# A long-convolution and feed-forward kernel: the last convolution step's loads move to GpSimd's queue and are untied from the weights' loads

## The chip, the cores and the metric

One Trainium2 chip, one core. A kernel's time is the device time of one launch in microseconds; the median of several runs is given. The profile is that of one further execution, with the hardware profiler on.

## The reference

The input `x` has 2048 positions of 576 features. It is normalised over the features, and the normalised rows go two ways; both results are added to `x`.

```python
xn = _layernorm(x, axis=-1)
return x + _A_ref(xn, ...) + _B_ref(xn, B_w1, B_w2)
```

`_A_ref` is a long convolution over the positions. Its kernel `K` (2048 taps for each feature) is a sum over 128 complex exponentials; the convolution is done with transforms of twice the length, and `u * Dskip` is added. `_B_ref` is a feed-forward layer:

```python
h = jnp.einsum("bsd,df->bsf", x, w1)     # 576 -> 4608
h = _silu(h)
out = jnp.einsum("bsf,fd->bsd", h, w2)   # 4608 -> 576
```

## The kernel before

**The main stream** is the feed-forward layer (`ffn`). The positions are 16 tiles of 128 rows, `j` = 0 to 15, in two halves of eight; each half is two blocks of four tiles. The 4608 hidden features are 9 chunks (`NCH`) of four tiles of 128. For each half, chunk and block, `up` (L283 to L301) makes the hidden tiles `gh` and `gl` from `w1`, and `down` (L303 to L325) multiplies them with `w2` into `po` in PSUM (three buffers, pool `ps2`), which VectorE adds to the running result `acc[j]` (L320). Precision is kept by splitting each operand in a high and a low part, so each product is three matmuls, and each weight tile, once loaded, is split by ScalarE (high part) and VectorE (low part).

**Weights.** `load_w1` (L240) loads two hidden tiles of `w1` into `w1r`, of which there is one buffer, with three DMAs (L247 to L249); `split_w1` makes `w1h` (ScalarE, L260) and `w1l` (VectorE, L262). `load_w2` (L265, DMA at L269) loads one tile of `w2` into `w2r`, two buffers; `split_w2` makes `w2h` (L278) and `w2l` (L280). A table in `ffn` says after which step of a block the next chunk's weights are loaded and split. Apart from the first, all these loads are in SyncE's queue. A load whose buffer is still being read waits in the queue, and what stands behind it waits too.

**The side stream** (`side`) is the convolution, cut into steps that `weave` places between the steps of the main stream at given fractions of its length. The convolution's transforms end with `spectral`, which stores 32 slices `yo` of its result to the DRAM tensor `d2` (L705, GpSimd's queue). Every row block of `d2` that is read later has rows of all 32 slices, so the first read waits for the last store.

**The last convolution step** is what the change touches. For each tile `j`, `conv_load` (L757) reads 256 rows of `d2` into a tile `ys` of 128 partitions by 4 by 288 floats, with two DMAs of 64 partitions each (L761); there are 8 buffers of `ys` (`AHEAD + 2`, `AHEAD` being 6). `add_conv` (L764) multiplies `ys` with the small matrix `s4` into two PSUM tiles `py` (L774), and VectorE adds them to the destination (L780). For tiles 0 to 7 the feed-forward result had been put aside in DRAM (`dr0`, L323); `load_r0` (L714, DMA at L716) reads it back, two tiles at a time, into `r0` (the profile's `r`), four buffers; after `add_conv` of an odd tile, `store` writes the pair out with four DMAs in GpSimd's queue (L171). For tiles 8 to 15 `add_conv` adds to `acc[j]` directly, in `down` of the last chunk (L307 to L309).

**Order around the change.** `tail` (L710) lists its steps with their places: the loads for tiles 0 to 7 from 0.895 of the main stream on, each 0.0045 after the one before; the eight `last` steps, each with the load for a later tile, from 0.922 on. Each runs under `behind(pins["load"])`: the scheduler may issue the step's instructions only after the weights' load that was built last (`load_w1` and `load_w2` put their DMA there). Within an engine's queue the schedule is fixed when the kernel is built. Each of SyncE's and GpSimd's kinds of DMA has eight semaphores in turn, so a DMA also waits until the eighth DMA before it in its kind has landed.

Of the kernel before, what the change touches and what calls it, by code (L numbers as in the profile page):

```python
# [17 lines left out]
P = 128  # L18
# [23 lines left out]
def kernel(  # L42
# [21 lines left out]
    nc = tc.nc  # L64
    FT = 4
# [17 lines left out]
    dr0 = dram.tile([8 * P, D], F32, name="dr0")  # L83
# [48 lines left out]
    pins = {}  # L132

    def behind(ins):
        return tc.issue_after(ins) if ins is not None else nullcontext()
# [32 lines left out]
    def store(t, j, engines):  # L168

        for ps, v, eng in quarters(ov, engines):  # L170
            eng.dma_start(v[:, j:j + 2] if len(t.shape) > 2 else v[:, j], t[ps])  # L171
# [61 lines left out]
    def ffn():  # L233
        w2v = w2.rearrange("(t p) d -> p t d", p=P)
# [5 lines left out]
        def load_w1(half, c, t):  # L240

            f = c * FT + t
            first = half == 0 and c == 0
            r1 = (pa if first and t else wp).tile([P, 5, 2 * P], F32, tag="w1r", name="w1r", bufs=1)
            fs = slice(f * P, (f + 2) * P)
            eng = nc.gpsimd if first and t == 0 else nc.sync
            eng.dma_start(r1[:, 0:4, :], w1[0:512, fs].rearrange("(k p) f -> p k f", p=P))  # L247
            eng.dma_start(r1[0:64, 4, :], w1[512:576, fs])
            pins["load"] = eng.dma_start(r1[64:128, 4, :], w1[512:576, fs]).ins  # L249
            R1[half, c, t] = r1  # L250

        def split_w1(half, c, t):
# [12 lines left out]
        def load_w2(half, c, t):  # L265

            first = half == 0 and c == 0
            r2 = (pa if first and t > 1 else wp).tile([P, D], F32, tag="w2r", name="w2r", bufs=2)
            pins["load"] = nc.sync.dma_start(r2, w2v[:, c * FT + t, :]).ins  # L269
            R2[half, c, t] = r2  # L270

        def split_w2(half, c, t):
# [30 lines left out]
        def down(blk, jj):  # L303
            half, c, b = blk
            j = 8 * half + 4 * b + jj
            js = slice(jj * P, (jj + 1) * P)
            if half == 1 and c == NCH - 1:  # L307
                conv_load(j + AHEAD)
                add_conv(j, acc[j])  # L309
            for h in range(2):  # L310
                hs = slice(h * HD, (h + 1) * HD)
                po = ps2.tile([P, 512], F32, tag="ps2", name="po")
                n = 0
                for t in range(FT):
                    for g, w in ((0, 0), (0, 1), (1, 0)):
                        pins["pe"] = nc.tensor.matmul(po[:, :HD], G[blk, t][g][:, js], W2[half, c, t][w][:, hs],  # L316
                                                      start=n == 0, stop=n == 3 * FT - 1).ins
                        n += 1
                with tc.high_priority():
                    nc.vector.tensor_add(acc[j][:, hs], po[:, :HD], acc[j][:, hs])  # L320
            if half == 0 and c == NCH - 1:
                rows = slice(j * P, (j + 1) * P)
                nc.sync.dma_start(dr0[rows, :], acc[j])  # L323
                if j % 2:
                    acc[7 + j], acc[8 + j] = load_x(7 + j, accp, "acc", (nc.sync,))  # L325
# [21 lines left out]
        for t in (0, 2):  # L347
            load_w1(0, 0, t)
        for t in (0, 2):
            split_w1(0, 0, t)  # L350
        for t in range(FT):
            load_w2(0, 0, t)
# [10 lines left out]
        for i, blk in enumerate(blocks):  # L363
            half, c, b = blk
            later = i + 1 < len(blocks)
            new = (half, c + 1) if c + 1 < NCH else (half + 1, 0)
            more = new[0] < 2
            if half == 0 and c == NCH - 1:
                next_xt(b)

            after = {
                (0, "u0"): [(load_w1, 0)],
                (0, "u1"): [(split_w1, 0), (load_w2, 0), (load_w2, 1)],
                (0, "u2"): [(load_w1, 2)],
                (1, "u0"): [(split_w1, 2), (split_w2, 0), (load_w2, 2)],
                (1, "d3"): [(split_w2, 1), (load_w2, 3), (split_w2, 2)],
                (1, "u2"): [(split_w2, 3)],
            }
            for step in ("u0", "d0", "d1", "d2", "d3", "u1", "u2", "u3"):
                k = int(step[1])  # L380
                if step[0] == "d":
                    down(blk, k)
                    yield 3.0
                elif later:
                    up(blocks[i + 1], k)
                    yield 3.0
                for f, t in after.get((b, step), ()) if more else ():
                    f(*new, t)
                if half == 0 and c == NCH - 1:
                    for kt in {"d3": (0, 1), "u1": (2, 3), "u2": (4,)}.get(step, ()):  # L390
                        split_xt(b, kt)
# [318 lines left out]
    def tail():  # L710

        r0s = {}

        def load_r0(j):  # L714
            r0s[j] = yp.tile([P, 2, D], F32, tag="r0", name="r0", bufs=4)
            nc.sync.dma_start(r0s[j], dr0[j * P:(j + 2) * P, :].rearrange("(i p) d -> p i d", p=P))  # L716

        def last(j):
            conv_load(j + AHEAD, 8)
            add_conv(j, r0s[j - j % 2][:, j % 2, :])  # L720
            if j % 2:
                store(r0s[j - 1], j - 1, (nc.gpsimd,))

        steps, at = [], tail_at[0]
        for j in range(8):
            for f in (conv_load, load_r0)[:2 - j % 2]:
                steps.append((at, f, j))
                at += tail_at[1]
        steps += [(tail_at[2] + j * tail_at[3], last, j) for j in range(8)]
        for at, f, j in sorted(steps, key=lambda v: v[0]):  # L730
            yield at
            with behind(pins["load"]):
                f(j)

    yss = {}

# [20 lines left out]
    def conv_load(j, first=0):  # L757
        if first <= j < NJ:
            yss[j] = yp.tile([P, 4, HD], F32, tag="ys", name="ys", bufs=AHEAD + 2)
            for h in range(2):  # L760
                nc.sync.dma_start(yss[j][64 * h:64 * h + 64],  # L761
                                  d2[j * 256:(j + 1) * 256, h * HD:(h + 1) * HD].rearrange("(q r) d -> r q d", q=4))

    def add_conv(j, dst):  # L764

        ys = yss.pop(j)
        py = [pss.tile([P, 512], F32, tag="pss", name="py") for _ in range(2)]
        first = pins["pe"]
        for n in range(8):
            q1, q2, h = n // 4, n // 2 % 2, 1 - n % 2  # L770
            o = 64 * q1 + 32 * q2
            rows = slice(64 * h, 64 * h + 64)
            with tc.high_priority() if n else nullcontext(), behind(first):
                mm = nc.tensor.matmul(py[h][o:o + 32, :HD], s4[rows], ys[rows, 2 * q2 + q1],  # L774
                                      start=True, stop=True, tile_position=(64 * h, o), skip_group_check=True)
            if n == 0:
                first = mm.ins
        for h in range(2):
            hs = slice(h * HD, (h + 1) * HD)
            nc.vector.tensor_add(dst[:, hs], py[h][:, :HD], dst[:, hs])  # L780
# [5 lines left out]
    def side():  # L786
# [40 lines left out]
        with tc.tile_pool(name="kl", bufs=2) as kl:  # L827
            for at in spectral():
                yield marks[1] + (at - 1) * (marks[2] - marks[1])
        yp = ctx.enter_context(tc.tile_pool(name="yp", bufs=3))  # L830
        yield from tail()

    sd = side()
# [87 lines left out]
```

## Time and profile before

| | |
|---|---|
| Median of three runs | 1129.19 us (1126.59 to 1129.72) |
| Profiled execution, its own time | 1131.96 us |
| Span of the profile, first to last instruction | 1130.2 us |
| Instructions | 22881 |
| Granted TensorE clock, mean | 0.996 of full speed |
| TensorE matmul busy | 1106.7 us, 98% |
| VectorE, ScalarE, GpSimd busy | 917.1, 708.7, 78.5 us |
| DMA queue q1 (SyncE), share of the 16 engines | 37.6%, 112.07 MB |
| DMA queue q0 (GpSimd), share | 9.4%, 34.14 MB |
| `ys` loads, `r` loads | 32 of 288 KB, 4 of 576 KB |

The profile names engines PE (TensorE), PEld (its weight loads), DVE (VectorE), ACT (ScalarE), POOL (GpSimd) and SP (SyncE). Register, branch, semaphore and DMA-issuing instructions are not counted as busy. A tile name stands without its buffer number, `out<-in`. All times inside a run are counted from the span's start. "SPq" and "POOLq" are the queues of the two engines that issue DMAs; an issue's time is the time the issuing engine takes over it, not that of the transfer. In the queue views, `q1 hardware_dynamic` is what SyncE issued and `q0 software_dynamic` what GpSimd issued; the columns are packets, MB and the share of 16 engines' time. Releasers are inferred: a wait for several things is put down to the last.

The moved DMAs run from 1028.5 to 1091.9 us of the span, its last tenth.

### The profile page before, as it was taken

To read this page: it belongs to the slowest core of one execution; us is meant where nothing else is said; L and a number is where in the kernel's file an instruction comes from. 1 tells how busy PE (TensorE), PEld (TensorE's weight loads), DVE (VectorE), ACT (ScalarE), POOL (GpSimd) and SP (SyncE) were. 2 spreads that over 40 slices of the span, in tenths; PEclk is the share of its full clock that TensorE was granted. 3 is DMA by queue.
4 is the path that set the end of the run, shared out by engine and by line. 5 is a ranking of instruction groups with operands and counts; after the bars stand their busy time and mean duration, and the time that the engine had idled before them with its cause. 6 is when DMAs were issued, how large, how long until landed. Compare 5 with 4: busy or idle time off the path is not lost.

```text
span 1130.2 us, 22881 instructions
## 1 busy us (share of the span) xinstructions
PE 1106.7 (98%) x9144; PEld 998.7 (88%) x9144; DVE 917.1 (81%) x1545; ACT 708.7 (63%) x1229; POOL 78.5 (7%) x130
## 2 busy tenths in 40 slices
PE   6999899999999999999999999999999999999998
PEld 5988799898888989999889998999999999998776
DVE  6698899999999999999999936887778778774433
ACT  4665356767677676676766727787777787772211
POOL 1110100000000000010000000000000000000110
PEclk9999899999999999999999999999999999999999
DMA  9346531334242625254743345554445455336971
GB/s 272 116 121 173 150 86 57 82 107 106 93 105 70 145 65 116 83 124 153 205 152 88 88 86 170 168 164 130 144 142 168 128 169 149 110 104 168 251 189 56
DMA packets 174971, 148.56 MB, mean 131 GB/s; under 512 B 110944, under 2 KB 141680, under 8 KB 174736
## 3 DMA queue, kind: packets, MB, share of 16 engines
q1 hardware_dynamic: 164768, 112.07, 37.6%
q0 software_dynamic: 9712, 34.14, 9.4%
q8 instruction: 72, 1.18, 0.4%
q10 hardware_dynamic: 384, 0.89, 0.3%
q14 instruction: 35, 0.29, 0.1%
HBM read 102.53 MB, written 44.61 MB: 130 GB/s over the span
## 4 chain that ended last, share of the span: by engine, by line
PE 86%; DVE 5%; DMA 5%; SPq 1%; issue 1%; ACT 0%; POOL 0%; DVEq 0%; POOLq 0%; ACTq 0%
PE po L316 36%; PE ph L291 30%; PE kp L631 3%; PE ph L292 3%; PE ph L293 2%; PE pk L754 2%; PE pu L754 2%; PE pb L754 2%; DMA w1r<-in_B_w_dram 2%; PE z L646 2%; PE pu L153 1%; DMA xj<-in_A_u_dram 1%; PE py L774 1%; PE pu L154 1%; DMA d1k<-stage 1%
## 5 line engine op out<-in xcount | busy, mean ns | idle before, releaser
L316 PE MATMUL po<-w2h,gh 128*128 128x288 f32 x1152 | 338.8, 297 | 6.4 <-DVE acc L320 5.7
L316 PE MATMUL po<-w2h,gl 128*128 128x288 f32 x1152 | 338.5, 297 | 1.0 <-DVE gl L301 1.0
L316 PE MATMUL po<-w2l,gh 128*128 128x288 f32 x1152 | 339.4, 296 | 0.0
L316 PEld LDWEIGHTS po<-w2h,gh 128*128 128x128 f32 x1152 | 216.1, 188 | 16.5 <-DVE acc L320 7.0
L316 PEld LDWEIGHTS po<-w2l,gh 128*128 128x128 f32 x1152 | 216.8, 188 | 4.3
L316 PEld LDWEIGHTS po<-w2h,gl 128*128 128x128 f32 x1152 | 216.5, 189 | 3.5 <-DVE gl L301 1.5
L299 ACT ACTIVATE gf<-ph 128x512 f32<-128x512 f32 (+1 forms) x148 | 86.5, 584 | 140.1 <-PE ph L293 124.7
L320 DVE TENSOR_TENSOR acc<-po,acc 128x288 f32<-128x288 f32 x288 | 126.3, 451 | 47.9 <-PE po L316 46.3
L291 PE MATMUL ph<-xh,w1h 128*128 128x512 f32 (+1 forms) x592 | 163.3, 391 | 0.5 <-ACT xh L123 0.5
L291 PE MATMUL ph<-xl,w1h 128*128 128x512 f32 (+1 forms) x592 | 161.5, 388 | 0.0
L291 PE MATMUL ph<-xh,w1l 128*128 128x512 f32 (+1 forms) x592 | 160.1, 386 | 0.0
L301 DVE TENSOR_TENSOR gl<-gf,gh 128x512 fp32r<-128x512 f32 (+1 forms) x148 | 98.7, 670 | 41.3 <-ACT gh L300 40.6
L291 PEld LDWEIGHTS ph<-xh,w1l 128*128 128x128 f32 x592 | 108.5, 189 | 20.1
L291 PEld LDWEIGHTS ph<-xl,w1h 128*128 128x128 f32 x592 | 108.5, 190 | 19.7
L291 PEld LDWEIGHTS ph<-xh,w1h 128*128 128x128 f32 x592 | 106.0, 191 | 20.0 <-issue 3.3
L300 ACT CAST gh<-gf 128x512 fp32r<-128x512 f32 (+1 forms) x148 | 89.5, 609 | 13.4 <-PE po L316 10.5
L278 ACT CAST w2h<-w2r 128x576 fp32r<-128x576 f32 x72 | 46.9, 672 | 30.6 <-PE po L316 19.5
L588 ACT ACTIVATE c<-th,magic 128x1040 f32<-128x1040 f32 x36 | 42.0, 1166 | 33.7 <-DVE C L611 25.7
L262 DVE TENSOR_TENSOR w1l<-w1r,w1h 128x640 fp32r<-128x640 f32 x72 | 56.9, 819 | 4.4 <-ACT w1h L260 4.3
L280 DVE TENSOR_TENSOR w2l<-w2r,w2h 128x576 fp32r<-128x576 f32 x72 | 53.4, 750 | 7.4 <-ACT w2h L278 7.2
L590 ACT ACTIVATE c<-th 128x1040 f32<-128x1040 f32 x36 | 38.7, 1076 | 32.6 <-DVE th L589 32.6
L292 PE MATMUL ph<-x,w1h 128*128 128x512 f32 (+1 forms) x148 | 57.2, 386 | 0.0
(182 smaller groups left out, 1836.9 us busy)
## 6 DMA issues: line engine op xcount, KB each, us to landing
w2r<-in_B_w_dram SPq DMA_DIRECT2D x72, 288.0 KB, 3.4
w1r<-in_B_w_dram SPq DMA_DIRECT2D x35, 512.0 KB, 3.9
d1u<-u POOLq DMA_DIRECT2D x32, 288.0 KB, 2.5
d1k<-stage SPq DMA_DIRECT2D x18, 512.0 KB, 7.7
ur<-d1u SPq DMA_DIRECT2D x32, 288.0 KB, 3.9
kr<-d1k SPq DMA_DIRECT2D x32, 288.0 KB, 2.8
d<-yo POOLq DMA_DIRECT2D x32, 288.0 KB, 3.9
ys<-d SPq DMA_DIRECT2D x32, 288.0 KB, 10.5
```

The source lines that it names most:

```text
L262: pins["w1l"] = nc.vector.tensor_sub(l1, src, h1).ins
L278: pins["w2h"] = nc.scalar.copy(h2, r2).ins
L280: nc.vector.tensor_sub(l2, r2, h2)
L291: nc.tensor.matmul(ph, w[:, kt, :], v[:, kt, a:e], start=n + kt == 0, stop=False)
L292: nc.tensor.matmul(ph, h1[:, 4, :], x4[:, a:e], start=False, stop=False)
L299: nc.scalar.activation(gf, ph, AF.Silu)
L300: pins["gh"] = nc.scalar.copy(gh, gf).ins
L301: pins["gl"] = nc.vector.tensor_sub(gl, gf, gh).ins
L316: pins["pe"] = nc.tensor.matmul(po[:, :HD], G[blk, t][g][:, js], W2[half, c, t][w][:, hs], start=n == 0, stop=n == 3 * FT - 1).ins
L320: nc.vector.tensor_add(acc[j][:, hs], po[:, :HD], acc[j][:, hs])
L588: nc.scalar.activation(c65, th, AF.Identity, bias=magic)
L754: nc.tensor.matmul(dst, st, mv[:, hs], start=n == 0, stop=n == 3 * len(terms) - 1)
```

## The change

All 32 `ys` loads and the four `r0` loads are issued by GpSimd instead of SyncE. The steps of `tail` no longer run behind the last weights' load, and `load_w1` and `load_w2` no longer record it.

```diff
@@ load_w1
-            pins["load"] = eng.dma_start(r1[64:128, 4, :], w1[512:576, fs]).ins
+            eng.dma_start(r1[64:128, 4, :], w1[512:576, fs])
@@ load_w2
-            pins["load"] = nc.sync.dma_start(r2, w2v[:, c * FT + t, :]).ins
+            nc.sync.dma_start(r2, w2v[:, c * FT + t, :])
@@ tail
         def load_r0(j):
             r0s[j] = yp.tile([P, 2, D], F32, tag="r0", name="r0", bufs=4)
-            nc.sync.dma_start(r0s[j], dr0[j * P:(j + 2) * P, :].rearrange("(i p) d -> p i d", p=P))
+            nc.gpsimd.dma_start(r0s[j], dr0[j * P:(j + 2) * P, :].rearrange("(i p) d -> p i d", p=P))
...
             yield at
-            with behind(pins["load"]):
-                f(j)
+            f(j)
@@ conv_load
             for h in range(2):
-                nc.sync.dma_start(yss[j][64 * h:64 * h + 64],
+                nc.gpsimd.dma_start(yss[j][64 * h:64 * h + 64],
                                   d2[j * 256:(j + 1) * 256, h * HD:(h + 1) * HD].rearrange("(q r) d -> r q d", q=4))
```

In the schedule that is built, the order of instructions on TensorE, VectorE and ScalarE is the same before and after. On SyncE the 36 DMAs are gone and the weights' loads stand in the same order without them. On GpSimd they stand behind the last `yo` store, in the order they had on SyncE: sixteen `ys` loads with three `r0` loads between them, the fourth `r0` load, four `ys` loads, the stores of tiles 0 and 1, and then by turns four `ys` loads and the stores of two tiles.

## The prediction

> **What bounds the kernel now.** I read the page first, then who made TensorE wait, then the chain of waits around that place, SyncE's timeline, and the DMA queues in short windows. The page has:
>
> ```profile
> PE 1106.7 (98%) x9144; PEld 998.7 (88%) x9144; DVE 917.1 (81%) x1545; ACT 708.7 (63%) x1229; POOL 78.5 (7%) x130
> ```
>
> TensorE is the bound, so a moved load counts only where TensorE waits. TensorE's waits from 1000 us to the end are one line (total, times, longest):
>
> ```profile
> PE po L316 <- DVE acc L320: 2.0, 1, 2.0
> ```
>
> This is the cap on any gain: 2.0 us. All moved loads lie in this stretch. The chain of waits (start, length, what) shows where the 2.0 us come from:
>
> ```profile
> 1039.94 1.48 DVE w1l L262 x2
> 1041.42 0.02 issue
> 1041.43 0.38 SPq L247
> ...
> 1043.59 11.82 DMA w1r<-in_B_w_dram
> ...
> 1056.27 1.56 DVE w1l L262 x2
> 1057.83 0.38 DVE acc L320
> 1058.21 0.04 issue
> 1058.25 5.04 PE po L316 x36
> ```
>
> The last `w1r` load is issued when VectorE has freed its single buffer, lands at 1055.41, and VectorE stands behind the split of it (`w1l`), so the `acc` add that frees a `po` buffer comes late. From landing to TensorE's restart it is 1058.25 - 1055.41 = 2.84 us. TensorE ran out of work at 1056.27. So with X for the landing, the stall is X + 2.84 - 1056.27 = X - 1053.43, never below nothing, and today 1.98 us. Everything in this prediction turns on X.
>
> Why did that load take 12 us? SyncE's timeline:
>
> ```profile
> 1034.17 3.81 SPq L761 DMA_DIRECT2D ys<-d  x4
> 1038.73 0.37 SPq L716 DMA_DIRECT2D r<-dr  x1
> 1041.43 0.38 SPq L247 DMA_DIRECT2D w1r<-in_B_w_dram  x1
> ...
> 1045.26 4.63 SPq L761 DMA_DIRECT2D ys<-d  x4
> 1058.89 0.35 SPq L269 DMA_DIRECT2D w2r<-in_B_w_dram  x1
> ```
>
> It stood in line behind `ys` and `r` loads of the same queue (landing 11.8 to 13.3 us after issue; the load before it, at 980.6 with nothing ahead, 3.2 to 3.8). In this stretch the DMA engines are full. Of 1070.5 to 1075 us, where only `ys` loads move, and of 1049.5 to 1051.5, where POOL's stores and this `w1r` share the engines, the queue view says:
>
> ```profile
> DMA packets 928, 1.02 MB, mean 226 GB/s; under 512 B 51, under 2 KB 927, under 8 KB 927
> ```
>
> ```profile
> q0 software_dynamic: 181, 0.55, 69.9%
> q1 hardware_dynamic: 223, 0.22, 32.3%
> ```
>
> The first is the speed of `ys` loads: 226 GB/s. The second is how two queues share: 223 packets of SyncE's to 181 of gpsimd's, 1.23 to one, though gpsimd's packets are 4608 bytes and `w1r`'s 1024. The turns go by packet, not by bytes.
>
> **The change, part by part.** *Queues.* 36 DMAs (32 `ys`, 4 `r`) leave SyncE and come to POOL. Each costs SyncE about 0.6 us (four in 2.80 us) and POOL 0.54 (128 rows, L705) to 0.77 (512 rows, L330), so 19 to 28 us of POOL in all, in a queue that is 7% busy: nothing, hidden by POOL's idle time. If that cover failed, the first loads would be late: `ys` 0 lands 4.0 us and `ys` 1 3.0 us before TensorE's `py` at 1037.65 and 1041.71. What POOL holds behind a waiting `ys` load are later `ys` loads and the stores of `r`, for which nobody waits; the tenth `ys` tile onward waits for an `add_conv` that is over 20 us ahead of its use. The order of TensorE's, VectorE's and ScalarE's instructions stays as it is, so `pins["load"]` costs nothing.
>
> *SyncE freed.* It no longer has `ys` loads waiting behind `w2r`'s buffer from 1049.9 to 1058.9, so `ys` 5 and later come earlier. TensorE does not wait for `ys` today, so this gains nothing; what it does is keep the DMA engines full past 1056, where today they run empty (5 tenths busy and less).
>
> *The two `w2r` loads (1058.89, 1068.35).* The first landed in 2.9 us on idle engines and is cast at 1066.8. Now it shares with `ys`: by the terms below 2.9, a wait of 3.7, and 2.7 for 8 rows in 6.5 turns of 0.42 us, 9.3 us together, so 1.4 us late; ScalarE's next work is at 1071.37, four idle microseconds that cover it. The second took 12.8 us in line and now takes about 9: earlier, and TensorE wasn't waiting. Both: nothing.
>
> *The `w1r` load.* Its issue time is set by VectorE and stays 1041.43. It no longer stands behind SyncE's line, but the same transfers now fill gpsimd's queue. Four terms:
> 1. On idle engines, from first issue to last landing (980.56 to 984.72): 4.2 us.
> 2. A wait for what the engines have already taken from the other queue. POOL's four stores at 1044.5 to 1046, issued into SyncE's backlog, landed after 6.4 to 6.9 us; like stores alone take 2.9 to 3.1. So 3.7 us; the other three groups give 1.0 to 5.9.
> 3. Sharing: 640 packets of 1024 bytes, 40 for each of 16 engines, alone some 0.05 us each (2.0 us, in term 1). At 1.23 to one that is 32.5 turns, in each of which a gpsimd packet goes through. gpsimd's queue puts several rows in one packet: between 6.0 and 9.9 us, when it carried a `w1r` load of 1024-byte rows, it shows 203 packets for 0.65 MB, 3.2 KB on average with the 4-byte semaphore writes counted in. For `ys`, four rows of 1152 make 4608 bytes. At 226 GB/s over 16 engines that takes 0.33 us; 32.5 x (0.33 + 0.06) - 2.0 = 10.7 us.
> 4. Sum: X = 1041.4 + 4.2 + 3.7 + 10.7 = 1060.0; the stall is 6.6 us, 4.6 more than now.
>
> No row of before shows a `ys` load on gpsimd's queue, so the bounds: a packet at 0.18 us, as POOL's stores take in the shared window (0.55 MB are 119 packets of 4608 bytes in 69.9% of 16 engines for 2.0 us), gives 32.5 x 0.24 - 2.0 = 5.8 and X = 1055.1 (0.3 us less than now); without term 2 as well, X below 1053.43, the stall gone, 2.0 us gained. At 0.95 to one (543 to 544.5 us: 112 to 118) and 5.9 in term 2, sharing costs 42 x 0.38 - 2.0 = 13.9, X = 1065.4 and 10.0 us are lost. I take 0.33 us, since the bytes, the partitions and the engines are those of the `ys` loads that ran at 226 GB/s.
>
> The Trainium skill, "DMA: Bandwidth & Descriptors", in "Queues, rings and completion order", says that each DMA engine goes round the queues and drains one whole packet from each, typically 9 to 17 descriptors. That turns go by packet is what 223 to 181 shows; that SyncE's packet holds some 13 rows the trace does not: its records are of one row. By that figure the 40 rows would need 3 or 4 turns, which is the first rival.
>
> **Rivals.** *The stall goes.* SyncE's queue gets several rows per turn, or gpsimd's packets hold one row. With one row (0.082 us at 226 GB/s) sharing costs 40 x 0.132 - 2.0 = 3.3 us; X = 1052.6, below 1053.43. For it: POOL's four stores, 0.59 MB against `w1r`'s 0.66, needed 7.8 to 10.4 us from first issue to last landing in a full queue, and 1041.4 + 10.4 = 1051.8. Against it: those were 8 packets for each engine, not 40. It decides when X falls under 1053.43; then 2.0 us are gained: 1131.96 - 1.98 = 1129.98 profiled, 1127.2 as a median.
>
> *Same place in line.* All transfers are served as they were issued. POOL, too, keeps 8 DMAs under way (`ys` landings are 12.2 us from issue, at 1.31 us each), so at 1041.4 it has issued 15 moved loads where SyncE had issued 13: two more, 2.6 us, X = 1058.0, 2.6 us lost: 1131.8. For it: the `dr` store of 538.2 took 7.5 us behind a gpsimd load, and from 540.5 to 542.5 only q0 moved. Against it: POOL's stores of 1044.5 landed before the `w1r` issued 3 us ahead of them. The Trainium skill, "DMA: Bandwidth & Descriptors", in "Issuing engines are not separate DMA queues", says that DMAs of different issuing engines run on the same 16 engines and interleave, so that another issuer saves only issue time. The shared window agrees that they interleave; by the rule the time would stay near this rival's.
>
> *`ys` late.* If gpsimd's queue carried `ys` at under some 140 GB/s, the first four tiles (about 3.5 MB with their `r`) would miss `py` at 1053.8, and TensorE would wait on `ys` itself. At 120 GB/s 3.5 MB take 29.5 us from 1029.8, 5.5 us too long; with the `w1r` wait hidden in it that is 1131.96 + 5.5 - 2.0 - 2.8 = 1132.7, and more at lower rates. Nothing in the trace shows such a rate; gpsimd's stores share at full speed, and POOL's issues keep to 0.54 us beside a VectorE that is 81% busy.
>
> **How the numbers follow.** The profiled execution took 1131.96 us, span 1130.2 and 1.8 around it; the median of the runs is 1129.19, 2.8 less, and I carry that difference over. Forecast: 1131.96 + 4.57 - 2.77 = 1133.8. The runs lie between 1126.59 and 1129.72, 0.28% apart, so 0.3% (3.4 us) is about what can be told from no change: slower begins at 1132.6, which is X over 1058.8. Chances: slow sharing, X over 1058.8, 0.47; `ys` late 0.03; X between 1053.4 and 1058.8 (same place in line, or faster packets) 0.22; the stall gone 0.22; a gain over 0.3%, for which the trace has no place, 0.06 for what a trace of one execution may not show. So slower 0.50, same 0.44, faster 0.06. The range goes from the stall gone, 1127.2, with 0.3 for the runs' spread, to the upper bound 1131.96 + 10.0 - 2.77 = 1139.2. The slow case alone: 1132.6 to 1139.2.
>
> **What would show it.** Right: `w1r` issued near 1041 and landing 17 to 20 us later; TensorE's wait for the `acc` add near 6.6 us at the same place; q0 carrying the `ys` loads in packets of some 4.6 KB; no `py` waiting for `ys`; the span near 1134.8. Wrong in the sharing step: `w1r` landing within 12 us and no TensorE wait after 1000 us. Wrong in kind: TensorE waiting at `py`, or ScalarE at `w2h` with `po` late behind it.

## The result, and the profile after

The changed kernel takes 1138.03 us (median of five runs, 1137.34 to 1139.29); the kernel before, in the same comparison, 1129.3 us (1126.59 to 1131.12). The ratio is 1.008, its 95% interval 1.0063 to 1.0098: slower, by 8.7 us. The profiled execution took 1137.34 us, its span is 1135.6 us.

From here on, lines of the changed kernel below `tail` have numbers one lower than before: `conv_load`'s DMA is L760, `py` L773, the add of `py` L779.

The first line of the page (engine, busy time, share, instructions) shows that the work of TensorE did not change, though its span did:

```profile
PE 1106.8 (97%) x9144; PEld 999.3 (88%) x9144; DVE 917.3 (81%) x1545; ACT 708.9 (62%) x1229; POOL 101.4 (9%) x166
```

TensorE's waits from 1000 us to the end (total, times, longest) are still one line, the same one, 9.4 us where it was 2.0:

```profile
PE po L316 <- DVE acc L320: 9.4, 1, 9.4
```

The chain of waits around it (start, length, what):

```profile
1036.42 1.48 DVE w1l L262 x2
1037.91 0.02 issue
1037.92 0.38 SPq L247
...
1038.92 20.40 DMA w1r<-in_B_w_dram
1059.32 0.02 issue
...
1061.73 0.38 DVE acc L320
1062.11 0.04 issue
1062.15 6.87 PE po L316 x36
```

The chain has the same members as before. The load is issued in the same moment in which VectorE frees `w1r` (this execution is 3.5 us earlier at that point than the profiled one of before; it is so already at the last `yo` store, 1022.37 against 1025.88, ahead of the first moved load, and counted from the first `py` matmul the load is issued after 3.78 us in both). But it lands at 1059.32, 21.4 us after its first issue, against 14.0 us before (1041.43 to 1055.41). And the 36 matmuls behind the wait take 6.87 us against 5.04: they are the same matmuls, more slowly.

SyncE's timeline from 1024 to 1064 us, whole, shows that nothing stands ahead of the load in its own queue:

```profile
1037.92 0.38 SPq L247 DMA_DIRECT2D w1r<-in_B_w_dram  x1
1038.35 0.53 SPq L248 DMA_DIRECT2D w1r<-in_B_w_dram  x1
1038.92 1.12 SPq L249 DMA_DIRECT2D w1r<-in_B_w_dram  x1
1062.79 0.33 SPq L269 DMA_DIRECT2D w2r<-in_B_w_dram  x1
```

The 20 us were spent beside GpSimd's queue. In the queue view of 1038 to 1043 us there is not one packet of SyncE's, although all three DMAs had been issued by 1040; beside `q0` it has a single packet of instructions. Then they take turns. The columns are packets, MB and the share of 16 engines; first 1038 to 1043, then 1046 to 1056 us:

```profile
q0 software_dynamic: 335, 1.26, 104.4%
```

```profile
DMA packets 1006, 2.33 MB, mean 233 GB/s; under 512 B 131, under 2 KB 605, under 8 KB 1006
q0 software_dynamic: 502, 1.85, 81.9%
q1 hardware_dynamic: 504, 0.49, 24.2%
```

504 packets of SyncE's went beside 502 of GpSimd's, and they carried 0.49 MB beside 1.85. By the sizes, 131 of the 1006 packets are small semaphore writes, 605 - 131 = 474 are rows of 1024 bytes and 1006 - 605 = 401 are packets of 4608, which is 1.18 rows of `w1r` for each large packet (four rows of `ys`, or two of `r`).

The counts alone would also allow turns of several packets on both sides. The packet records of the trace speak against it. From 1046 to 1056 us the end of one packet of 4608 bytes is followed within 20 ns by the start of another 598 times, and at distances of 160 to 400 ns, which is chance, 618 times on average; for the `w1r` rows it is 911 against 864. From 1038 to 1043 us, when GpSimd's queue had the engines to itself, it was 906 against 574. So a side that has the engines to itself shows packets that follow one another, and two sides that share them do not: the turns are of one packet.

Why the matmuls were slower is in the windows (stretch, length, then busy time and count of PE, PEld, DVE, ACT and POOL, then the granted TensorE clock, DMA share, GB/s):

```profile
1055.00:1056.00 1.00, 0.00 (x0) 0.00 (x0) 0.00 (x0) 0.00 (x0) 0.00 (x0) 1.00 1.02 232
1056.00:1057.00 1.00, 0.00 (x0) 0.00 (x0) 0.00 (x0) 0.00 (x0) 0.53 (x1) 0.51 1.08 242
...
1065.00:1066.00 1.00, 1.00 (x6) 1.00 (x6) 0.46 (x1) 0.00 (x0) 0.71 (x3) 0.50 1.02 392
1066.00:1067.00 1.00, 1.00 (x9) 1.00 (x9) 0.00 (x0) 0.00 (x0) 1.00 (x2) 0.88 1.12 290
```

TensorE's last matmul ahead of the wait ended at 1052.76. From 1056.0 on, 3.3 us later, the granted clock is half, and it comes back at about 1066.2, some 4 us after the restart at 1062.15. That is 6.87 - 5.04 = 1.83 us more for the 36 matmuls. In the 2.0 us wait of before the clock stayed at 1.00. The Trainium skill, "TensorE: Matmul & The Clock Gate", Part 1 ("What's actually happening"), says that TensorE falls to half its rate after an idle window of about 3.4 us and needs about as long of sustained work to come back; the rows agree in kind, with 3.3 and 4.1 us.

So the time went to one place: 9.4 - 2.0 = 7.4 us more waiting and 1.8 us of half clock, 9.2 us, beside 8.7 between the medians. From the first issue of that load to the end of the span the profiles measure 88.8 us before and 97.7 after, 8.9 us more.

### The profile page after: what moved, and what is told of

Same layout as the page of the kernel before. It is cut to its first block, busy times and chain, and to the rows that moved or that the text cites. A ratio compares the mean times of both kernels' runs of the same rounds, so it can differ in the third digit from the quotient of the medians.

```text
span 1135.6 us, 22877 instructions
## 1 busy us (share of the span) xinstructions
PE 1106.8 (97%) x9144; PEld 999.3 (88%) x9144; DVE 917.3 (81%) x1545; ACT 708.9 (62%) x1229; POOL 101.4 (9%) x166
## 3 DMA queue, kind: packets, MB, share of 16 engines
q8 instruction: 72, 1.18, 0.4%
## 4 chain that ended last, share of the span: by engine, by line
PE 87%; DVE 5%; DMA 4%; SPq 1%; issue 1%; POOL 1%; ACT 0%; ACTq 0%; DVEq 0%; POOLq 0%
PE po L316 37%; PE ph L291 30%; PE kp L631 3%; PE ph L292 3%; PE ph L293 2%; PE pk L753 2%; PE pu L753 2%; PE pb L753 2%; DMA w1r<-in_B_w_dram 2%; PE z L646 2%; DMA xj<-in_A_u_dram 1%; PE pu L153 1%; DVE st L180 1%; PE py L773 1%; PE pu L154 1%; SPq L230 1%
## 5 line engine op out<-in xcount | busy, mean ns | idle before, releaser
L316 PE MATMUL po<-w2h,gh 128*128 128x288 f32 x1152 | 339.9, 298 | 14.2 <-DVE acc L320 12.7
L156 POOL DMA_DIRECT2D d1u<-u x32 | 17.4, 542 | 471.4 <-ACT u L155 471.4
```

## The experiments

**Theory.** The last `w1r` load, alone in SyncE's queue, first waits for what the DMA engines have taken from GpSimd's queue, and then gets one row of 1024 bytes in about each turn against 4608 of `ys`; VectorE stands behind its split, and TensorE behind VectorE. **Rivals:** the engines share by bytes, so that the rows' size does not matter; the load waits for the transfers that were issued before it, in whichever queue; the tie to the weights' loads was what held the order, and the queue did nothing.

"Stage" below is the time from the first `py` matmul of the last convolution step to the end of the span: 92.5 us before, 101.4 after. Ratios are to the kernel before.

**Rows of half the length** (label e4_half_rows). The changed kernel; the same bytes of the last `w1r` load in rows of 512.

```diff
-            eng.dma_start(r1[:, 0:4, :], w1[0:512, fs].rearrange("(k p) f -> p k f", p=P))
+            if half == 1 and c == NCH - 1 and t == 2:
+                for i in range(2):
+                    hs = slice(f * P + i * P, f * P + (i + 1) * P)
+                    ht = slice(i * P, (i + 1) * P)
+                    eng.dma_start(r1[:, 0:4, ht], w1[0:512, hs].rearrange("(k p) f -> p k f", p=P))
+            else:
+                eng.dma_start(r1[:, 0:4, :], w1[0:512, fs].rearrange("(k p) f -> p k f", p=P))
```

> The changed kernel, with the large part of the last w1r load issued as two DMAs of 512-byte rows in place of one of 1024-byte rows: the same bytes, 72 rows for each engine in place of 40. Turns by packet (my theory): 32 rows more at 1.25 to a gpsimd packet are 26 more turns of 0.38 us, 9.7 us; the load lands some 31 us after its issue (21.4 in the changed kernel), TensorE's wait for the acc add grows from 9.4 to about 19 us, and the time is near 1147.7. Shares by bytes (rival: SyncE's queue gets a fixed quarter of the bytes while gpsimd's is full): the bytes are the same, landing 21 to 22 us, time 1138 as the changed kernel.

Measured: 1145.2 us (1143.14 to 1147.71), ratio 1.0144 (1.0119 to 1.0168), stage 109.3. From first issue to last landing 28.1 us (1039.04 to 1067.15) instead of 21.4. The waits from 1000 us (lines are six lower down in this kernel), and the queue view of 1046 to 1056 us:

```profile
PE po L322 <- DVE acc L326: 16.0, 1, 16.0
```

```profile
DMA packets 1140, 2.43 MB, mean 243 GB/s; under 512 B 123, under 2 KB 675, under 8 KB 1140
q0 software_dynamic: 572, 2.14, 91.3%
q1 hardware_dynamic: 568, 0.28, 15.5%
```

The number of packets on both sides is again the same, while SyncE's bytes in the window fell from 0.49 to 0.28 MB; by data packets it is 552 of 512 bytes to 465 of 4608, 1.19 where it was 1.18. Here the engines take turns by packet, and on SyncE's queue a packet is one row. A fixed share by bytes is excluded. I had expected 31 us; a row of SyncE's now takes 0.044 us of an engine (15.5% of 16 engines for 10 us, by 568) where it took 0.077, so the turns are shorter.

**Only this load in GpSimd's queue** (e5_w1_alone). The kernel before, all `ys` and `r` loads in SyncE's queue and tied; the two queues of this one load against the others are exchanged.

```diff
-            eng = nc.gpsimd if first and t == 0 else nc.sync
+            eng = nc.gpsimd if first and t == 0 or half == 1 and c == NCH - 1 and t == 2 else nc.sync
```

> The kernel before, with the last w1r load alone in gpsimd's queue; the ys and r loads stay in SyncE's. Turns by packet: now the w1r has the large packets (10 of 4 KB for each engine) and ys the small ones (1152 bytes), so it needs 10 turns of about 0.3 us: 4.2 us on idle engines, some 4 for what is already taken, 2.8 for the turns, 11 us from issue to landing; X is 1052.5 in before's times, the stall is gone, 2.0 us are gained: 1127.3. Served in the order of issue (rival): it lands after 13.3 us as in the kernel before, TensorE waits 2 us: 1129.3.

Measured: landed 10.8 us after its first issue (1037.91 to 1048.71), no TensorE wait after 1000 us, stage 90.8. Time 1127.42 us (1125.79 to 1129.65), ratio 0.9992 (0.9979 to 1.0004): the gain of at most 2 us is not told from nothing by the time. The queue view of 1043 to 1048 us:

```profile
q1 hardware_dynamic: 409, 0.70, 52.9%
q0 software_dynamic: 261, 0.85, 52.4%
```

The load is now on the side of the large packets, beside `ys` and `r` loads in one row to a packet, and takes half the time that it takes on the other side. Its first packet moved at 1044.1, so that GpSimd's queue was empty in the first microsecond of this view; from 1044 to 1047 us the counts are 207 to 185. From its first packet to the end of its last, 1048.0, it needed 3.9 us for 160 packets of 4096 bytes, where its 640 rows needed 14.2 us in the changed kernel. That speaks for turns and against a place in one common line, which would have made it later than 10.8 us; the comparison by time alone would not have shown it.

**The tie alone** (e2_untied_sync). The kernel before without the tie, all loads still in SyncE's queue.

```diff
-            with behind(pins["load"]):
-                f(j)
+            f(j)
```

> One half of the change alone: the steps of tail are no longer tied behind the weights' loads, but the ys and r loads stay in SyncE's queue. (The other half alone, gpsimd's queue with the tie kept, builds the very schedule of the changed kernel, so the tie plays no part there.) In SyncE's line two more r loads and four more ys tiles now stand ahead of the last w1r load, about 8 of 1.31 us and 2.16 us, some 12 us, and the schedule itself puts w1l behind one more acc add. If the place in line is all (theory): the load lands 20 us or more after the time at which it landed in the kernel before less what SyncE's eight DMAs in flight allow, TensorE's wait grows to between 5 and 12 us, 1132 to 1141. If the loss were gpsimd's queue as such (rival): no TensorE wait beyond before's 2 us, 1128 to 1129.

Measured: 1138.46 us (1137.27 to 1140.26), ratio 1.0086 (1.0073 to 1.0099), stage 102.6: as slow as the whole change. Two pieces of SyncE's timeline, and the waits from 1000 us:

```profile
1035.39 12.00 SPq L760 DMA_DIRECT2D ys<-d  x8
1049.00 0.38 SPq L247 DMA_DIRECT2D w1r<-in_B_w_dram  x1
```

```profile
PE po L316 <- DVE acc L320: 10.1, 1, 10.1
```

Same victim, other road. Without the tie, eight `ys` loads stand ahead of the `w1r` load in SyncE's line, and they take 12.0 us to issue because each waits for an earlier `ys` or `r` load to land; the load is issued at 1049.00, lands at 1060.28, 11.3 us later, and the clock falls to 0.50 here as well. So the tie was what kept SyncE's line free for the weights. In GpSimd's queue it has nothing to keep free: with the loads there and the tie kept, the schedule that is built is that of the changed kernel, so it was not run. The trace of the changed kernel agrees: nothing stood ahead of the load in its queue. The two halves of the change are not two costs that add up: taking the tie away alone loses 9.6 us (1138.46 to 1128.82), moving the loads alone is the changed kernel and loses 8.7.

**A buffer of its own, issued early** (e6_w1x_after on the changed kernel, e8_w1x_before on the one before). The last `w1r` load gets a buffer `w1x` and is issued earlier, counted from the first `py` matmul by 13 us in the one and 10 us in the other, so VectorE's freeing of `w1r` no longer times it.

```diff
+            if half == 1 and c == NCH - 1 and t == 2:
+                r1 = yp.tile([P, 5, 2 * P], F32, tag="w1x", name="w1x", bufs=1)
+            else:
+                r1 = (pa if first and t else wp).tile([P, 5, 2 * P], F32, tag="w1r", name="w1r", bufs=1)
...
-                (0, "u0"): [(load_w1, 0)],
+                (0, "u0"): [(load_w1, 0)] + [(load_w1, 2)] * (new == (1, NCH - 1)),
...
-                (0, "u2"): [(load_w1, 2)],
+                (0, "u2"): [(load_w1, 2)] * (new != (1, NCH - 1)),
```

> The changed kernel with a buffer of its own for the last w1r load (w1x), which SyncE then issues with the first ys loads, 12 us earlier. Turns by packet (theory): it shares with a full gpsimd queue at once and takes 12 to 20 us, landing at 1038 to 1046, before VectorE comes to it at about 1048: no TensorE wait for an acc add, the loss and before's 2 us gone, 1126 to 1128; the first ys tiles come later by up to 2.6 us, with 3 us to spare. Rival (ys pushed late takes the place of it): TensorE waits at py for some microseconds, 1130 or more.

Measured: 1127.33 us (1125.38 to 1130.79), ratio 0.9984 (0.9973 to 0.9995), stage 89.9, no TensorE wait after 1000 us. The whole loss is gone with one load out of the way. The load took 6.2 us (1024.53 to 1030.77), less than I had expected: at that time GpSimd's queue had only begun (its first `ys` load was issued at 1025.38).

> The kernel before, with a buffer of its own for the last w1r load (w1x), so that it no longer waits for the split of the load before, and stands in SyncE's line behind the second ys tile instead of the fifth. Theory (the landing of this load is all that TensorE waits for here): it lands near 1042, no TensorE wait after 1000 us, 1129.3 - 2.0 = 1127.3. Rival (the wait is for the DMA engines as a whole, and something else, the ys tiles pushed back by 0.66 MB, 2.6 us, takes its place): TensorE waits at py, 1129.3 or more.

Measured: 1128.94 us (1125.19 to 1131.19), ratio 1.0004 (0.999 to 1.0018), stage 91.8. The load landed at 1037.13 and the wait for `acc` is gone, yet the 2.0 us are not in the time. What TensorE waits for after 1000 us now (lines are three higher in this kernel):

```profile
PE py L777 <- DMA ys<-d: 0.5, 1, 0.5
PE py L777 <- DVE r L783: 0.3, 1, 0.3
```

The load stands in SyncE's line between the first `ys` tiles, and 0.8 us come back as waits for the tiles behind it. The stage is 0.7 us shorter; why the median is not lower at all stays open, within an interval that allows a gain of 1.1 us. The time is nearer to the rival's than to the 1127.3 that I had expected.

**The split later** (e9_late_split on the changed kernel, e9b_late_split_before on the one before). The load stays as it is; its split is moved behind the `acc` adds in VectorE's queue.

```diff
-                with behind(pins["xt1"] if first else None):
+                with behind(pins["xt1"] if first else pins["acc"] if half == 1 and c == NCH - 1 and t == 2 else None):
...
-                    nc.vector.tensor_add(acc[j][:, hs], po[:, :HD], acc[j][:, hs])
+                    pins["acc"] = nc.vector.tensor_add(acc[j][:, hs], po[:, :HD], acc[j][:, hs]).ins
...
-                (1, "u0"): [(split_w1, 2), (split_w2, 0), (load_w2, 2)],
-                (1, "d3"): [(split_w2, 1), (load_w2, 3), (split_w2, 2)],
+                (1, "u0"): [(split_w2, 0), (load_w2, 2)] if new == (1, NCH - 1) else [(split_w1, 2), (split_w2, 0), (load_w2, 2)],
+                (1, "d3"): [(split_w1, 2)] * (new == (1, NCH - 1)) + [(split_w2, 1), (load_w2, 3), (split_w2, 2)],
```

> The changed kernel with its DMAs as they are; only VectorE's split of the last w1r load (and ScalarE's) is placed behind the acc adds of that block, so that a late load holds up no acc add. Theory (the loss is TensorE's wait for the acc adds behind w1l, and the half clock that followed it): the load still lands some 21 us after issue, TensorE does not wait, the granted clock stays 1.00, and the whole loss of 8.7 us and before's 2.0 us go: 1127.3. Rival (the ys loads in gpsimd's queue themselves slow the stage): some of the loss stays, 1130 or more.

Measured: 1125.87 us (1123.88 to 1127.68), ratio 0.9972 (0.9959 to 0.9985), stage 89.9: faster than both kernels. The windows from 1050 to 1065 us, columns as above:

```profile
1050.00:1055.00 5.00, 5.00 (x49) 4.38 (x48) 2.71 (x6) 0.00 (x0) 1.87 (x3) 1.00 1.05 238
1055.00:1060.00 5.00, 5.00 (x50) 4.37 (x49) 1.62 (x4) 0.00 (x0) 1.67 (x3) 1.00 1.06 294
1060.00:1065.00 5.00, 5.00 (x45) 4.18 (x45) 2.71 (x6) 1.93 (x3) 0.99 (x2) 1.00 1.03 233
```

The load is as slow as ever, 21.9 us (1039.40 to 1061.26), but TensorE is busy throughout at full clock. A late weight tile costs nothing by itself at this place; it costs because the order in VectorE's queue puts the split ahead of the `acc` adds that TensorE needs.

> The kernel before (all loads in SyncE's line) with the split of the last w1r load placed behind the acc adds. Theory: before's TensorE wait of 2.0 us is gone and nothing else changes: 2 us under the kernel before, and within 1 us of the changed kernel with the same edit (2.3 us under it). If the queues matter beyond this one load (rival), the two differ by more than that.

Measured: 1127.12 us (1126.16 to 1129.75), ratio 0.999 (0.998 to 1.0), stage 90.3, no TensorE wait after 1000 us. This is the 2.0 us that any change here could have won; 1.7 of them show against 1128.82, the median of before in that comparison, and the interval just reaches no change. With the split out of the way, the kernel with `ys` in GpSimd's queue has the lower median, by 1.25 us. That is a little over the 1 us that I had set for the rival, but the two medians come from two comparisons, whose kernels before differ by 0.7 us, the two intervals overlap, and the stages differ by 0.4: whether the queues matter beyond this load is not told by it. The loss of the change is not in the queue alone, but in the queue and the place of the split together.

**The load on ScalarE's queue** (e10_w1_act). The kernel before, with the last `w1r` load issued by ScalarE, beside `ys` in rows of 1152 bytes on SyncE's queue.

```diff
-            eng = nc.gpsimd if first and t == 0 else nc.sync
+            eng = nc.gpsimd if first and t == 0 else nc.scalar if half == 1 and c == NCH - 1 and t == 2 else nc.sync
```

> The kernel before with the last w1r load issued by ScalarE, so in a hardware queue of its own beside SyncE's full one: rows of 1024 bytes against rows of 1152, one row to a packet on both sides. Turns by packet (theory): 40 rows against 40 rows of about 0.08 us cost 3.3 us: 4.2 + 4 + 3.3 = 11.5 us from issue to landing, where beside gpsimd's 4.6 KB packets it took 21.4. Rival (any second queue starves the smaller transfer): 18 us or more, TensorE waiting as in the changed kernel. The time is less telling, since ScalarE also loses 1.2 us to the issues and the schedule moves two matmuls: 1126 to 1130 by the theory, 1135 or more by the rival.

Measured: from first issue to last landing 11.6 us (1043.97 to 1055.61), as expected. The queue view of 1048 to 1054 us (`q10` is ScalarE's queue):

```profile
q1 hardware_dynamic: 753, 0.82, 52.0%
q10 hardware_dynamic: 678, 0.65, 41.9%
q0 software_dynamic: 135, 0.39, 16.3%
```

Two queues with packets of one row each share about evenly in packets and in bytes, and the same load that needs 21.4 us beside packets of 4608 bytes needs 11.6 here. The time missed what I expected: 1132.98 us (1131.58 to 1133.71), ratio 1.0033 (1.0021 to 1.0045), stage 97.2. Counted from the first `py` matmul (1034.79 here, 1037.65 in before), the issue came 5.4 us later than in before and the landing 3.1 us later, since each of the three DMAs waited for an earlier `ys` landing: their semaphores are three of the eight that SyncE's loads use in turn. What stood behind the issues in ScalarE's own queue waited too:

```profile
1043.97 0.40 ACTq L247 DMA_DIRECT2D w1r<-in_B_w_dram  x1
1044.42 0.60 ACT L299 ACTIVATE gf<-ph 128x512 f32<-128x512 f32 x1 [7.02 <-DMA ys<-d]
```

TensorE's waits grew:

```profile
PE po L316 <- DVE acc L320: 2.9, 1, 2.9
PE py L774 <- DVE r L780: 1.2, 1, 1.2
PE ph L291 <- ACT gf L299: 1.0, 1, 1.0
```

These three are 5.1 us, 3.1 more than before's 2.0, beside the 3.7 us that the ratio makes. The wait for `gf` comes from those 7.0 us. The one at `py` comes at 1084 us from the last `w2r` load, for which ScalarE waits 7.6 us (5.4 in before) and whose split stands ahead of the add to `r` in VectorE's queue; why that load is later was not followed. The load in ScalarE's queue had a price of its own, and so the time does not decide between theory and rival; the landing does.

## Why the prediction was right, and where its sizes were off

**The mechanism held.** The forecast was 1133.8 us, with 0.50 on slower; the kernel came out at 1138.03, in the upper part of the range and of the slow case. TensorE waits at the same place for the same `acc` add, `w1r` is issued when VectorE frees it, `q0` carries `ys` in packets of 4608 bytes, and no `py` waits for `ys`. That the stall is X - 1053.43, counted from the issue, held to a tenth: landing came 2.8 us later after the issue than forecast (21.4 to 18.6), and the stall is 9.4 instead of 6.6.

**Term 1, idle engines, 4.2 us.** The size holds: the load before the last one took 4.1 us in the changed kernel (977.05 to 981.13). Of the 4.2 us in before, 1.1 lie ahead of the first packet (981.6), 2.7 in the packets and 0.4 behind the last (984.3); beside the full queue it was 1.5 us from the end of the last packet, 1057.8, to the landing at 1059.32, 1.1 more. Why is open.

**Term 2, what the engines have already taken, 3.7 us.** The first packet of `w1r` went at 1043.6, 5.7 us after the issue, of which 1.1 are the same on idle engines: 4.6 us. The term was real and 0.9 too small, inside its bounds of 1.0 to 5.9. That it comes with the other queue's backlog is shown by the early load of `w1x` on the changed kernel, whose first packet went 1.0 us after the issue; what the engines hold during the wait no run shows.

**Term 3, sharing, 10.7 us.** The rows moved in 14.2 us (1043.6 to 1057.8), alone in 2.7: 11.5 us, so the term was 0.8 too small. The ratio in it was 1.23 to one with the small packets counted in; counted alike it was 1.00 here, so that 40 rows took 40 turns and not 32.5. The turn was a little shorter than 0.39 us: 81.9% and 24.2% of 16 engines for 10 us, divided by 502 and 504 packets, make 0.26 and 0.08 us, 0.34 together, and 40 of these are 13.5 us of the 14.2. The two errors go in opposite directions, so that the sum came out near was in part luck. The rule that a packet typically holds 9 to 17 descriptors (the Trainium skill, "DMA: Bandwidth & Descriptors", "Queues, rings and completion order") would by the prediction's estimate have made it 3 or 4 turns; the windows and the half rows show one row in each of SyncE's packets.

**The term that was missing** is the clock. The sum ended with TensorE's restart, as if the matmuls behind a stall of 6.6 us ran like those behind one of 2.0. They cost 1.8 us more. The prediction read TensorE's waits from 1000 us on, where none is long enough to show it. Earlier, the profile of before does show it (the second of TensorE's waits up to 1028 us, and the window from 125.1 to 131.8 us):

```profile
PE po L316 <- DVE acc L320: 3.7, 1, 3.7
125.10:131.80 6.70, 6.03 (x24) 5.80 (x24) 6.70 (x14) 4.04 (x7) 3.15 (x1) 0.50 0.43 176
```

A wait of 3.7 us, which ended at 123.81, had 6.8 us of half clock behind it, and the forecast stall of 6.6 us was longer than that wait. The sum put at nothing a term that its own trace had.

**The base.** To carry over the 2.8 us by which the profiled execution of before lay above its median was the same as to count from the median, and that was right: 2.8 us of later landing and 1.8 of clock are 4.6, and the median came out 4.2 above the forecast. The span near 1134.8, at 1135.6, is nearly right for the wrong reason: the profiled execution of after was 3.5 us ahead when the load was issued, and the stall and the clock took that back. The difference of the two spans, 5.4 us, would have hidden the missing term; the stage from the issue to the end, 8.9 us, shows it.

**What was costed at nothing.** The two `w2r` loads landed 5.9 and 5.0 us after issue, below the 9.3 and 9 forecast, and TensorE did not wait for them. POOL is busy 22.9 us more (78.5 to 101.4), within the 19 to 28, unseen elsewhere. The `ys` loads took a median of 7.5 us from issue to landing where it was 10.5, and this won nothing. "`pins["load"]` costs nothing" is right for the change as made, and no more: in SyncE's queue the tie was worth 9.6 us, as its removal alone shows.

**The rivals.** "The stall goes" needed several rows in SyncE's packet or one in GpSimd's; neither is so. "Same place in line" gives 1131.8 and a landing 16.6 us after the issue; it was 21.4, and `ys` loads that were issued after it (1041.19 to 1045.09) landed before it (1054.07 to 1058.98), so there is no common line. "`ys` late" did not show: no wait at `py`.

## What to carry to other kernels

Before moving bulk loads to another queue, look which small urgent load will run beside them: here the DMA engines took turns by packet, so the load with short rows in a packet each fell to its share of packets, not of bytes, and being alone in its queue didn't help it. Ask then what stands behind its consumer: here one pair of splits ahead of the `acc` adds in VectorE's queue made the late load cost 9 us, and moving the splits made it cost nothing (ratio 0.9972). For a stall that is longer than those that your trace shows at full clock (2.9 us here), add the half clock behind it (1.8 to 2.7 us here), and look for its sign in the whole trace, not only near the change. Judge a difference between profiles by the stage, not by the span of one execution.

## What the runs showed of the hardware that was not expected

- TensorE's granted clock fell to half 3.3, 4.2 and 4.9 us after the last matmul and came back 4.1, 4.4 and 6.0 us after the restart (the changed kernel, the tie alone, the half rows); the matmuls behind the wait took 1.8, 2.1 and 2.7 us more. So neither time is fixed. Waits of 2.0 and 2.9 us left the clock at 1.00. All ten profiles have a wait of 3.1 to 3.7 us for an `acc` add that ends near 123 us, with 3.4 or 6.8 us of half clock behind it.
- Between the queues of SyncE and GpSimd the packets went one to one over 10 us, 504 to 502 with rows of 1024 bytes and 568 to 572 mostly with rows of 512, whatever their bytes.
- For 5.7 us after its issue (1.1 us on idle engines) a load in an otherwise empty queue moved nothing, while the other queue kept all 16 engines busy.
- SyncE's and ScalarE's DMAs took their semaphores from the same eight, so ScalarE's issue of one load, and its own work behind it, waited for SyncE's `ys` landings (7.0 us).
